# Scores of two heads at once over half of TensorE's rows, w1's row factors applied after the product, and filler products ahead of gelu

## The chip, the cores and the metric

One core of a Trainium2 chip runs the kernel. The metric is the device time of one execution in microseconds, median of several runs; the core's span in the profile is 1.7 to 2.9 us shorter. A run on one core has no die to compare with, so "fast" means within 1.5% of the fastest run of the same kernel.

## The reference, cut to what matters

```python
B, S, D, H, F = 1, 2048, 640, 32, 1536            # 32 heads of 20 columns
xn = layernorm(A_x)
q, k, v = heads(xn @ wqkv)
p = softmax(q @ k^T * 20**-0.5)                    # 32 x 2048 x 2048 exponentials
s = concat(p @ v) @ wo
h  = gelu(layernorm(xn) @ w1)                      # branch B, tanh gelu
x1 = xn + shift(h) @ w2                            # four column groups shifted by 1, -1, 2, -2 rows
g  = silu(x1 + gelu(layernorm(x1) @ w3) @ w4)
return A_x + s * g
```

The 32 x 2048 x 2048 exponentials are nearly all of the work. ScalarE takes most of them, in tiles of 128 x 1024; VectorE takes the rest by a bit trick on 16-bit integers (the "blocks" below).

## The kernel before: what the change and the argument touch

The kernel's instruction order is fixed when it is built. A planner walks through time; each task has an engine, a booked duration and a due time, and a ready task is put where the engine's booked time is free. Each engine is then given its list in that order.

TensorE's products here are of a column mode (128 rows, 32 columns; `128*32` or `128*22` in the profile) or of a row mode (32 rows, 128 columns; `32*128`). In the trace of the kernel before, a column group of four matmuls starts about 0.215 us after another one (though one matmul lasts 0.38 us by its modelled end), but 0.31 to 0.32 after a row-mode score; and two column groups ahead of a row-mode score need 0.55 us where two take 0.43. These extra times, about 0.11 us on entry and 0.10 on exit, are what "drain" stands for. The planner books what a change of mode costs:

```python
self.mode_cost = 100.0
...
            t.finish = st + t.dur
            if e == "pe":
                if t.mode != pe_mode:          # charged on entry and on exit
                    t.finish += self.mode_cost
                pe_mode = t.mode
...
def c_pe(ninstr, N):
    return ninstr * max(14.0, 0.106 * N)       # four column matmuls of 512: 217 ns
```

The scores of one ScalarE tile (two heads, 128 keys, 512 queries) are, from the second group on, eight column matmuls against zero-padded queries QM. They are booked at 440 ns. Each tile is followed by one exponential:

```python
        def fn(e):
            for jj in range(2):
                ...
                for c in range(4):
                    ins = e.matmul(out[32*c:32*c+32, :], self.KT[:, b, 128*kt + 32*c:128*kt + 32*c + 32],
                                   self.QM[:, gb, 2*a + jj, :], ..., tile_position=(0, 32 * c))
        T("pe", 220 if gb is None else 440, fn, ..., mode=int(gb is None), cls=-1, acq=("S", hs))
        return self.exp_act(hs, sa)
```

Before w1's products the kernel multiplies the whole transposed input by the row factors, one VectorE instruction of 5 x 516 columns for each of four chunks. The products are then copied out of PSUM:

```python
            T("dve", c_dve(KC * 516, "1x"), fy, ..., name=f"y2_{ch}")
            ...
                T("dve", c_dve(512), lambda e: e.tensor_copy(hx[:, ch, m, :], self.wbank(h)[:, 0:512]), ...)
```

`DUE` holds due times of the side work (projections, branch B), and `ND` says how many blocks of each group of 512 queries VectorE takes. Both were tuned for this planner.

## Time and profile before

| | before |
|---|---|
| time, median of 4 (range) | 890.98 us (888.92 to 891.34) |
| exponentials on ScalarE | 836 |
| first one starts, last one ends, tail | 36.3, 878.1, 11.3 us |
| granted TensorE clock, mean | 0.992 |

The lines that carry it are in the prediction below.

How to read ScalarE's rate: neighbouring exponentials overlap (one lasts 1036 ns in the profile). The busy time of their group counts overlap once, so busy time over count (779.9 / 836 = 0.933 us) is what one costs on average. If an exponential comes a little late, the overlap shrinks and the busy time per exponential grows, while the idle column shows nothing; the changed kernel below has 24.8 us of this.

### The profile page before, as it was taken

The page shows a single profiled execution, that of the slowest core. Times are in us where ns is not written, and L with a number is a line of the kernel's source. Part 1 is how long each engine was busy: PE and PEld are TensorE (multiplying, and loading weights), DVE is VectorE, ACT ScalarE, POOL GpSimd, SP SyncE. Part 2 cuts the span into 40 slices and gives each one's busy share as a digit, 9 for nine tenths or more (in the row PEclk, how much of TensorE's full clock was granted, in tenths as well). Part 3 has the DMA queues.
Part 4 walks back from the last instruction along what each step waited for, and adds up shares of the span by engine and source line. Part 5 has one row for each costly group of instructions (what it writes and reads, how often), then busy time and mean ns, then how long its engine had stood idle before and what let it go on. Part 6 is the DMA issues. An engine that isn't in the chain of part 4 may idle for free.

```text
span 889.4 us, 34152 instructions
## 1 busy us (share of the span) xinstructions
PE 829.2 (93%) x15630; PEld 364.1 (41%) x15630; DVE 724.4 (81%) x1000; ACT 851.0 (96%) x900; POOL 37.8 (4%) x69
## 2 busy tenths in 40 slices
PE   4999999999999999999998999999999799998996
PEld 2434333334444433344443544433434344444453
DVE  7756888887888899989776779987878679797895
ACT  6899999999999999999998999999999999999994
POOL 7310000000000000000000000000000000010000
PEclk9999999999999999999999999999999999999998
DMA  6003300012210013222223031222222201114322
GB/s 222 11 14 87 94 22 25 25 43 77 80 48 29 22 46 86 62 61 57 62 53 98 20 95 35 72 84 59 54 60 51 82 10 53 47 53 126 105 63 76
DMA packets 83548, 54.81 MB, mean 62 GB/s; under 512 B 52556, under 2 KB 77340, under 8 KB 83276
## 3 DMA queue, kind: packets, MB, share of 16 engines
q1 hardware_dynamic: 83404, 52.62, 21.1%
q8 instruction: 123, 2.02, 0.9%
q14 instruction: 21, 0.17, 0.1%
HBM read 37.91 MB, written 10.63 MB: 55 GB/s over the span
## 4 chain that ended last, share of the span: by engine, by line
ACT 45%; PE 27%; DVE 19%; DMA 8%; issue 1%; SPq 0%
ACT arena L1404 42%; PE psum L771 11%; PE psum L1380 8%; DVE arena L1345 4%; DVE arena L1431 4%; DMA arena<-recips 4%; PE psum L1362 3%; PE psum L1319 3%; PE psum L1354 2%; DMA recips<-arena 2%; DVE arena L970 2%; DMA queries<-arena 1%; ACT arena L1756 1%; ACT arena L1698 1%; DVE arena L1682 1%
## 5 line engine op out<-in xcount | busy, mean ns | idle before, releaser
L1404 ACT ACTIVATE arena<-psum 128x1024 bf16<-128x1024 f32 x836 | 779.9, 1036 | 16.5 <-PE psum L1362 5.6
L1380 PE MATMUL psum<-arena 128*32 128x512 bf16 x4992 | 380.0, 381 | 11.5 <-ACT arena L1404 9.5
L771 PE MATMUL psum<-arena 128*32 128x320 bf16 (+1 forms) x5952 | 360.3, 335 | 7.8 <-DVE arena L1161 3.5
L1431 DVE TENSOR_SCALAR arena<-psum 128x1024 uint16<-128x1024 f32 x188 | 229.1, 1218 | 52.9 <-PE psum L1362 51.8
L1345 DVE TENSOR_SCALAR arena<-arena 128x4096 uint16<-128x4096 uint16 (+1 forms) x236 | 230.1, 1008 | 5.4 <-PE psum L1354 4.1
L771 PEld LDWEIGHTS psum<-arena 128*32 128x32 bf16 x5952 | 147.9, 97 | 148.0 <-issue 27.4
L1380 PEld LDWEIGHTS psum<-arena 128*32 128x32 bf16 x4992 | 106.8, 95 | 145.6 <-ACT arena L1404 102.6
L1319 PE MATMUL psum<-arena 128*22 128x512 bf16 x1672 | 161.6, 381 | 2.0 <-DVE arena L1466 1.7
L1354 PE MATMUL psum<-arena 128*22 128x512 bf16 x1504 | 123.3, 380 | 2.1 <-DVE arena L1345 1.9
L1362 PE MATMUL psum<-arena 32*128 32x512 bf16 x800 | 83.7, 386 | 14.3 <-ACT arena L1404 6.6
L1319 PEld LDWEIGHTS psum<-arena 128*22 128x22 bf16 x1672 | 42.4, 92 | 54.2 <-issue 7.5
L1362 PEld LDWEIGHTS psum<-arena 32*128 32x128 bf16 x800 | 21.4, 91 | 98.8 <-ACT arena L1404 81.7
L1354 PEld LDWEIGHTS psum<-arena 128*22 128x22 bf16 x1504 | 36.4, 92 | 45.5 <-DVE arena L1345 10.6
L1753 DVE CAST arena<-psum 128x512 bf16<-128x512 f32 x48 | 33.0, 687 | 14.1 <-PE psum L771 14.1
L1205 DVE CAST arena<-psum 128x512 bf16<-128x512 f32 x40 | 27.3, 685 | 18.1 <-PE psum L771 18.1
L1479 DVE TENSOR_TENSOR arena<-arena 128x512 bf16<-128x512 f32 x28 | 19.3, 689 | 16.1 <-DMA arena<-recips 15.8
L1550 DVE SCALAR_TENSOR_TENSOR arena<-psum,arena 128x320 bf16<-128x320 f32 x32 | 15.5, 487 | 15.4 <-PE psum L771 15.4
L970 DVE BATCH_NORM_STATS2 arena<-arena 128x6 f32<-128x320 bf16 x52 | 23.0, 482 | 2.8 <-DMA arena<-in_A_x_dram 2.8
L1466 DVE COPY arena<-psum 128x512 f32<-128x512 f32 x28 | 19.2, 687 | 3.6 <-PE psum L1354 2.8
L1767 DVE TENSOR_TENSOR arena<-psum,arena 128x320 bf16<-128x320 f32 x32 | 15.5, 485 | 6.8 <-PE psum L771 6.8
L1756 ACT ACTIVATE arena<-arena 128x12288 bf16<-128x12288 bf16 x2 | 20.9, 10444 | 0.0
L1069 PE MATMUL psum<-arena 128*32 128x128 bf16 x320 | 9.3, 246 | 12.2 <-DVE arena L984 11.8
(101 smaller groups left out, 281.2 us busy)
## 6 DMA issues: line engine op xcount, KB each, us to landing
arena<-in_B_w_dram SPq DMA_DIRECT2D x48, 160.0 KB, 2.6
arena<-recips SPq DMA_DIRECT2D x28, 256.0 KB
arena<-arena SPq DMA_DIRECT2D x124, 32.0 KB, 1.9
arena<-in_B_w_dram SPq DMA_DIRECT2D x4, 960.0 KB, 5.3
arena<-in_A_x_dram SPq DMA_DIRECT2D x8, 320.0 KB, 6.1
arena<-in_A_x_dram SPq DMA_DIRECT2D x16, 160.0 KB, 2.5
out_dram<-arena SPq DMA_DIRECT2D x16, 160.0 KB, 1.8
arena<-keys SPq DMA_DIRECT2D x28, 80.0 KB
```

What stands on the lines that cost most here:

```text
L771: ins = e.matmul(pb[32 * c:32 * c + 32, 0:N], lhsT(k, c), rhs(k, c), start=(k == 0), stop=(stop and k == nk - 1), tile_position=(0, 32 * c))
L970: lambda e, li=li, n=n, hh=hh: e.bn_stats(st[:, li, 6 * hh:6 * hh + 6], xn[:, n, hD * hh:hD * hh + hD]),
L1205: T("dve", c_dve(512), lambda e, h=h, c=c: e.tensor_copy(KS[:, 512 * c:512 * c + 512], self.wbank(h)[:, 0:512]), reads=[wa], writes=[A("KS ...
L1319: ins = e.matmul(pb[32 * i:32 * i + 22, 0:512], VA[:, ql, kts[i // 2], i, :], PT[:, slots[i // 2][0].slot, 512 * (i % 2):512 * (i % 2) + 512],
L1345: T("dve", c_dve(w, "4x"), lambda e, v=v, dst=dst: e.tensor_scalar(dst, U[:, ub, 0:w], 0.5, EXP_B[v], op0=ALU.mult, op1=ALU.add), reads=ha ...
L1354: ins = e.matmul(pb[32 * i:32 * i + 22, 0:512], wv, dst[:, at:at + 512].bitcast(BF16), start=first, stop=final, tile_position=(0, 32 * i))
L1362: return e.matmul(out, self.KT[32 * i:32 * i + 32, b, 128 * kt:128 * kt + 128], self.QT[32 * i:32 * i + 32, b, 512 * qc:512 * qc + 512], s ...
L1380: ins = e.matmul(out[32 * c:32 * c + 32, :], self.KT[:, b, 128 * kt + 32 * c:128 * kt + 32 * c + 32], self.QM[:, gb, 2 * a + jj, :], start ...
L1404: lambda e: e.activation(self.PT[:, hp.slot, :], self.psum[:, 512 * hs.slot:512 * hs.slot + 1024], AF.Exp, scale=cfg.scale),
L1431: ins = e.tensor_scalar(U[:, ub, 1024 * at + 512 * k:1024 * at + 512 * k + w], self.psum[:, 512 * hd.slots[k]:512 * hd.slots[k] + w], a_ex ...
L1753: T("dve", c_dve(512), lambda e, h=h, fc=fc, i=i: e.tensor_copy(GT[:, i, fc, :], self.wbank(h)[:, 0:512]), reads=[wa], writes=at, name=f"g ...
L1756: T("act", 2750 + c_act(2 * FC * 512), lambda e: e.activation(GT[:, :, :, :], GT[:, :, :, :], AF.Gelu_apprx_tanh), reads=gta, writes=gta, ...
```

## The change

Its intent: halve the matmul time of ScalarE's scores by running two heads at once, each over 64 of the 128 rows; take the four long row-factor products off VectorE by multiplying when w1's products are evicted anyway; keep TensorE's clock up around the gelus with 24 filler products (before, the stretch from 702 to 710 us, after the third gelu, has a granted clock of 0.79); move more blocks to VectorE and some layer-norm tiles to GpSimd. The planner's bookings of transfers and of mode switches are altered, and all due times are retuned. Left out of the cut below are other booked times of transfers, the places of the blocks in groups with four of them (`UNITS`), and the loading of the row factors, which is now one transfer of 256 KB for each of the 20 evictions in place of one of 1 MB. Cut to its core:

```diff
-                if t.mode != pe_mode:
+                if pe_mode and not t.mode:              # a switch is charged on leaving a row mode only
                     t.finish += self.mode_cost
...
-        self.dma_bw = 280.0
+        self.dma_bw = 223.0
-            k0=-37.9, k1=-9.1, ...                      # all due times
+            k0=216.0, k1=-160.6, ...
+        self.POOLN = [6, 7, 8, 12]                      # norm tiles on GpSimd
-        self.FALL = False
+        self.FALL = True
+        self.FILL = 8                                   # fillers ahead of each of three gelus
-            [2, 2, 3, 3], [3, 3, 3, 3], ...             # ND: 94 blocks on VectorE
+            [1, 2, 3, 3], [3, 3, 3, 4], ...             # 101 blocks
...
+    def score_half(self, b, qc, kt, a, gb):
+            for jj in range(2):
+                r = slice(64 * jj, 64 * jj + 64)
+                ins = e.matmul(self.bank(hs.slot + jj)[:, :], self.KT[r, b, 128 * kt:128 * kt + 128],
+                               self.QM[r, gb, a + 2 * jj, :], ..., tile_position=(64 * jj, 0))
+        T("pe", 220, fn, ..., mode=1, cls=-1, acq=("S", hs))
...
-            T("dve", c_dve(KC * 516, "1x"), fy, ...)
-                T("dve", c_dve(512), lambda e: e.tensor_copy(hx[...], self.wbank(h)[:, 0:512]), ...)
+                T("dve", c_dve(512), lambda e: e.tensor_tensor(hx[...], self.wbank(h)[:, 0:512], RR[:, r, :], op=ALU.mult), ...)
+        self.fill("g1", at)                             # 8 x 16 matmuls, also ahead of the two gelus of w3
```

## The prediction

> **What bounds the kernel now.** I read the page's busy shares first, then its slices, then the groups by line and shape, then the waits, the chain of waits in order of time, and last a close timeline of TensorE.
>
> ```profile
> span 889.4 us, 34152 instructions
> PE 829.2 (93%) x15630; PEld 364.1 (41%) x15630; DVE 724.4 (81%) x1000; ACT 851.0 (96%) x900; POOL 37.8 (4%) x69
> ...
> PE   4999999999999999999998999999999799998996
> ...
> ACT  6899999999999999999998999999999999999994
> ```
>
> ScalarE is the bound: 96% busy, and full in all but the first two slices and the last. TensorE reads 93%, but matmul ends are modelled with the pipeline's tail, so its real slack must come from a timeline.
>
> ```profile
> L1404 ACT ACTIVATE arena<-psum 128x1024 bf16<-128x1024 f32 x836 | 779.9, 1036 | 16.5 <-PE psum L1362 5.6 <-PE psum L1319 5.1 <-PE psum L1380 4.2
> L1380 PE MATMUL psum<-arena 128*32 128x512 bf16 x4992 | 380.0, 381 | 11.5 <-ACT arena L1404 9.5
> L1431 DVE TENSOR_SCALAR arena<-psum 128x1024 uint16<-128x1024 f32 x188 | 229.1, 1218 | 52.9 <-PE psum L1362 51.8
> L1345 DVE TENSOR_SCALAR arena<-arena 128x4096 uint16<-128x4096 uint16 x140 | 167.5, 1226 | 3.0 <-PE psum L1354 2.3
> ```
>
> These are groups (busy us, mean ns, then idle before them). The 836 exponentials last 1036 ns each but overlap: 779.9 / 836 = 0.933 us apiece. With ScalarE's other late work (gelu 8.7 + 20.9, tanh 10.1, six table loads of 1.28 = 7.7, all from the groups) the list after the first exponential is 828.2 us. The first exponential starts at 36.3 (timeline), the last ends at 878.1 (ScalarE is busy for 3.1 of the window 875 to 880), so 11.3 us of tail follow. 36.3 + 828.2 + 11.3 = 875.8; the other 13.6 us are waits of ScalarE in the middle, close to the 14.9 that the group line gives to TensorE's lines. These are what a schedule can win back, and I want to know what causes them.
>
> ```profile
> 126.29 2.75 DVE arena L1682
> 129.04 1.14 DVE arena L1345
> 130.18 1.13 DVE arena L1431
> 131.32 0.17 DVE arena L1473
> 131.49 0.02 issue
> 131.50 3.08 DMA recips<-arena
> 134.58 0.02 issue
> 134.59 5.06 DMA arena<-recips
> 139.66 0.02 issue
> 139.68 0.69 DVE arena L1479
> ```
>
> This is the chain in order of time (start, length). VectorE, which runs its list in order, does a 2.75 us row-factor product (L1682), then its list stands until a reciprocal has gone out to memory and come back; ScalarE then misses 0.6 and 0.2 us near 144. The same two transfers stand ahead of its gaps near 193, 476, 586 and 656. In total VectorE loses this much to them:
>
> ```profile
> DVE arena L1479 <- DMA arena<-recips: 15.8, 12, 3.9
> ```
>
> [...]
>
> ```profile
> 50.31 0.39 PE L1362 MATMUL psum<-arena 32*128 32x512 bf16 x2
> 50.63 0.62 PE L771 MATMUL psum<-arena 128*32 128x512 bf16 x8
> 51.18 0.39 PE L1362 MATMUL psum<-arena 32*128 32x512 bf16 x2
> 51.49 0.40 PE L1319 MATMUL psum<-arena 128*22 128x512 bf16 x4
> 51.72 0.39 PE L771 MATMUL psum<-arena 128*32 128x512 bf16 x4
> ```
>
> Four column matmuls of 512 take about 0.215 us start to start. Two row matmuls side by side need 0.31 to 0.32 before the next column group starts (50.31 to 50.63), and two column groups ahead of a row group need 0.55 instead of 0.43 (50.63 to 51.18). One visit to a row mode thus costs about 0.11 on entry and 0.10 on exit. [...] TensorE waits 3.5 us before 696.9, and the granted clock of the window 702 to 710 is 0.79.
>
> **The change part by part.**
> Scores. A tile was 8 column matmuls, two rounds of four, 0.43 us; 624 of them are 268 us. Now it is two matmuls over 64 rows side by side, one round of 0.21, but in a row mode. In the built order 520 of the 592 such tiles stand alone between column work, and row-mode visits go from 210 to 751. Cost: 592 x 0.21 + 541 x 0.22 = 243 us. The halving of the matmul time is given back to drains: a lone tile costs 0.21 + 0.21 = 0.42 against 0.43. TensorE gains 25 us, mostly because there are 32 fewer such tiles.
> Added on TensorE: 16 more row groups of the shared tiles (3.4), 21 more value groups (21 x 0.215 = 4.5), 24 fillers of 16 matmuls (96 x 0.215 = 20.6). Sum +28.5: TensorE's work is a few us more, not less. Gelu waits for the last filler, but they are laid between scores ahead of it, so they cost slots, not a block.
> Exponentials. The blocks given to VectorE go from 94 to 101, so ScalarE has 14 fewer exponentials: 14 x 0.933 = 13.1 us, straight off the path. This is the largest sure gain.
> VectorE. 14 more evictions (17.1), 20 more wide pieces (20 x 1.226 = 24.5), 16 fewer narrow ones (16 x 0.689 = 11.0), four row-factor products of 2.83 gone (-11.4), two norm tiles gone (-0.9). Sum +18.3: 743 us, about 85% of the new span. The factor itself is free: it rides on an eviction that reads PSUM anyway (0.69 us either way).
> Prologue. 15 fewer value groups of 320 columns (0.137 each, 2.05 us) stand before the first score, where TensorE is nearly solid. Four norm tiles go to GpSimd, which may delay its own last powers. I take 1.3 us of the 2.05: first exponential at 35.0.
> Schedule. The planner's times for the small transfers and the bandwidth are corrected, and the big lump on VectorE is gone. The five stall sites named above sum to about 6 us (0.75, 0.7, 2.5, 0.4, 1.5); I expect most of it to go.
>
> **The sum.** Waits in the middle: 13.6 - 6 (transfers, lump) - 1.5 (clock near the third gelu) + 3.5 (VectorE and TensorE are denser) = 9.6. Then 35.0 + (828.2 - 13.1) + 11.3 + 9.6 = 871.0 us of span; the timed median is 1.3 above the profiled span before, so 872. I lean 1 us lower, as the due times were retuned with everything else: 871.
>
> **Rivals.**
> First, TensorE becomes cheaper than I say, because a switch to 64 rows drains less than one to 32 rows. For it: the planner now charges the switch on leaving only. Against it: the drain before 51.18 is on entry. If only 0.32 us were paid per tile, TensorE would gain 60 us, the waits would fall to about 5, and the time to about 866.
> Second, VectorE takes over as the bound. Counting the built order from the 200th to the 418th exponential (means as above, less 0.06 for the overlap of neighbours), VectorE has about as much work as ScalarE's 203 us there, from long runs with four blocks per group; before, the same count for exponentials 251 to 420 gives 91%, which matches 92% busy in 300 to 400. Against it: at 95% busy from 300 to 340 ScalarE lost nothing. If it bites, waits grow by 8 or so and the time is about 880.
> Third, TensorE is the bound, since nothing was taken from it and the span shrinks. By the same count it needs 48.4 us for exponentials 101 to 150, where ScalarE takes 46.7, and 50.7 against about 50.5 for 451 to 500. That would cost 3 to 6 us: 875 to 878.
>
> **Range and chances.** The floor with no waits at all is 35.0 + 815.1 + 11.3 + 1.3 = 863; the second and third rival together give about 884. Eight times in ten within 862 to 882. The line for "faster by over 2%" is 872.9, close to my sum, so it is little better than even: 0.55 faster, 0.43 the same, 0.02 slower.
>
> **What would show it right or wrong.** The exponentials: 822 at about 0.933, ScalarE near 837 busy. The half-row tiles: about 0.42 us from the start of such a tile's predecessor's end to the next column group, and TensorE's in-stream load not lower; if the next column group starts 0.21 after one, I was wrong on the drains. VectorE's waits for the reciprocals should fall well below 15.8. The clock at the gelus should stay near 1. VectorE's busy share between 230 and 430 us should be over 95%; if ScalarE's idle time sits there, the second rival is right. The prediction is wrong altogether if the first exponential starts later than before, or if ScalarE's waits in the middle rise above 13.6.

## More of the kernel before

Booked times that are wrong do not break the result. They produce an order that fits another machine.

One more view is needed as a measure for later, the share of each engine in the chain of waits that ended last:

```profile
ACT 45%; PE 27%; DVE 19%; DMA 8%; issue 1%; SPq 0%
```

ScalarE leads the chain. TensorE and VectorE each hold it for part of the span.

## The result, and the profile after

The changed kernel takes 917.82 us (914.84 to 919.08, four runs) against 890.98. The ratio is 1.030, with a 95% interval from 1.027 to 1.033: slower by 3%. All ratios here are those of the mean times of fast runs and not of the medians quoted beside them.

The page of the changed kernel (busy shares, three engines' slices, chain of waits by engine, the group of the exponentials):

```profile
PE 833.8 (91%) x12354; PEld 285.9 (31%) x12354; DVE 744.3 (82%) x1018; ACT 860.7 (94%) x884; POOL 44.7 (5%) x74
...
PE   4899999999899999988989999898996898989996
...
ACT  5799999999999999999999999899999899999995
...
PE 67%; ACT 24%; DVE 5%; DMA 3%; issue 1%; POOL 1%; SPq 1%; ACTq 0%
...
L1444 ACT ACTIVATE arena<-psum 128x1024 bf16<-128x1024 f32 x822 | 791.6, 1033 | 27.7 <-PE psum L1398 8.6
```

ScalarE still looks full, yet the chain has turned from ScalarE to TensorE (27% before, 67% after). TensorE's total busy time hardly moved (829.2 to 833.8). The group line explains where the time is: 822 exponentials take 791.6 us, 0.963 each instead of 0.933. At the old rate they would have taken 766.8.

The span grew by 23.7 us in the profiled runs. In terms of these lines: the first exponential starts 1.1 later (37.4); 14 exponentials fewer save 13.1; the stretched busy time costs 791.6 - 766.8 = 24.8; idle time ahead of exponentials rises by 11.2; the tail is 0.5 shorter. The sum is +23.5.

So the larger loss does not show as idle time at all. To see it I counted, from the trace's start times, the interval from one exponential to the next where nothing lies between them on ScalarE. Back to back it is 903 to 905 or 919 to 921 ns (584 of the 824 intervals before, 396 of 810 after), and never less than 903. Before, 128 intervals lie between 0.96 and 1.10 us; after, 340 do. I call these "small late" ones. All that intervals of up to 1.10 us have above 0.925 sums to 11.3 us before and to 40.9 after: 29.6 us of waits of which the page shows few as idle. What longer gaps have above 0.925 went from 18.5 to 22.3. The granted clock does not explain the small late ones: by the trace's clock records TensorE ran at half clock for 17 us between the first and the last exponential (7 us before), and none of the 340 lies there.

Where they come from is seen in TensorE's timeline (start, length, instruction; L1388 is a row-mode score, L1398 a half tile, the other lines are column work):

```profile
62.75 0.39 PE L1388 MATMUL psum<-arena 32*128 32x512 bf16 x2
63.07 0.83 PE L782 MATMUL psum<-arena 128*32 128x512 bf16 x12
63.84 0.39 PE L1388 MATMUL psum<-arena 32*128 32x512 bf16 x2
64.15 0.40 PE L1345 MATMUL psum<-arena 128*22 128x512 bf16 x4
...
153.93 0.39 PE L1398 MATMUL psum<-arena 64*128 64x512 bf16 x2
154.25 0.83 PE L782 MATMUL psum<-arena 128*32 128x512 bf16 x12
155.01 0.39 PE L1398 MATMUL psum<-arena 64*128 64x512 bf16 x2
155.33 0.40 PE L1345 MATMUL psum<-arena 128*22 128x512 bf16 x4
```

From one score to the next it is 1.09 and 1.08 us: 0.32 for the score and the switch behind it, then three column groups and the switch ahead of the next score, 0.76. ScalarE could have taken the next tile after 0.91. The planner booked 0.22 + 0.10 for such a tile, and three groups at 0.217: 0.97. It believed that three groups nearly fit into the time of one exponential. They don't. Of the 399 exponentials that start over 0.95 us after the one before, I found the score of 393 to be a row-mode tile with TensorE's work solid up to it.

### The profile page after: what moved, and what is told of

Read it like the earlier page. It is cut to its first block, busy times and chain, and to the rows that moved or that the text cites. A ratio compares the mean times of both kernels' runs of the same rounds, so it can differ in the third digit from the quotient of the medians.

```text
span 913.1 us, 27675 instructions
## 1 busy us (share of the span) xinstructions
PE 833.8 (91%) x12354; PEld 285.9 (31%) x12354; DVE 744.3 (82%) x1018; ACT 860.7 (94%) x884; POOL 44.7 (5%) x74
## 3 DMA queue, kind: packets, MB, share of 16 engines
q1 hardware_dynamic: 86336, 56.82, 22.3%
## 4 chain that ended last, share of the span: by engine, by line
PE 67%; ACT 24%; DVE 5%; DMA 3%; issue 1%; POOL 1%; SPq 1%; ACTq 0%
PE psum L782 25%; ACT arena L1444 19%; PE psum L1398 15%; PE psum L1345 10%; PE psum L1380 8%; PE psum L1388 6%; PE psum L1749 2%; DVE arena L1471 2%; DMA arena<-in_B_w_dram 2%; ACT arena L1810 1%; ACT arena L1738 1%; DMA arena<-in_A_x_dram 1%; ACT arena L1826 1%; DMA queries<-arena 0%; ACT arena L1016 0%
## 5 line engine op out<-in xcount | busy, mean ns | idle before, releaser
L1444 ACT ACTIVATE arena<-psum 128x1024 bf16<-128x1024 f32 x822 | 791.6, 1033 | 27.7 <-PE psum L1398 8.6
L782 PE MATMUL psum<-arena 128*32 128x320 bf16 (+1 forms) x5952 | 348.9, 336 | 6.0 <-DMA arena<-in_B_w_dram 1.4
L1471 DVE TENSOR_SCALAR arena<-psum 128x1024 uint16<-128x1024 f32 (+1 forms) x204 | 246.5, 1209 | 61.2 <-PE psum L1388 60.0
L1371 DVE TENSOR_SCALAR arena<-arena 128x4096 uint16<-128x4096 uint16 (+1 forms) x244 | 247.0, 1036 | 6.8 <-PE psum L1380 5.8
L1398 PE MATMUL psum<-arena 64*128 64x512 bf16 x1184 | 230.7, 387 | 10.1 <-ACT arena L1444 9.3
L782 PEld LDWEIGHTS psum<-arena 128*32 128x32 bf16 x5952 | 139.4, 96 | 122.2 <-issue 49.9
L1380 PE MATMUL psum<-arena 128*22 128x512 bf16 x1616 | 128.9, 381 | 0.6 <-DVE arena L1371 0.5
L1398 PEld LDWEIGHTS psum<-arena 64*128 64x128 bf16 x1184 | 56.6, 92 | 216.3 <-ACT arena L1444 119.4
L1388 PE MATMUL psum<-arena 32*128 32x512 bf16 x864 | 90.4, 385 | 31.6 <-ACT arena L1444 26.3
L1388 PEld LDWEIGHTS psum<-arena 32*128 32x128 bf16 x864 | 23.1, 91 | 109.3 <-ACT arena L1444 77.2
L1380 PEld LDWEIGHTS psum<-arena 128*22 128x22 bf16 x1616 | 34.2, 90 | 35.7 <-issue 16.8
L1749 PE MATMUL psum<-arena 128*32 128x512 bf16 x384 | 25.1, 381 | 0.5 <-DVE arena L1225 0.5
L1286 DVE CAST arena<-psum 128x320 bf16<-128x320 f32 x32 | 15.4, 488 | 8.8 <-PE psum L782 8.7
L1519 DVE TENSOR_TENSOR arena<-arena 128x512 bf16<-128x512 f32 x28 | 19.1, 684 | 2.8 <-DMA arena<-recips 2.7
L1089 PE MATMUL psum<-arena 128*32 128x128 bf16 x320 | 8.9, 247 | 13.4 <-DVE arena L999 10.6
```

The source lines that it names most:

```text
L782: ins = e.matmul(pb[32 * c:32 * c + 32, 0:N], lhsT(k, c), rhs(k, c), start=(k == 0), stop=(stop and k == nk - 1), tile_position=(0, 32 * c))
L1371: T("dve", c_dve(w, "4x"), lambda e, v=v, dst=dst: e.tensor_scalar(dst, U[:, ub, 0:w], 0.5, EXP_B[v], op0=ALU.mult, op1=ALU.add), reads=ha ...
L1380: ins = e.matmul(pb[32 * i:32 * i + 22, 0:512], wv, dst[:, at:at + 512].bitcast(BF16), start=first, stop=final, tile_position=(0, 32 * i))
L1388: return e.matmul(out, self.KT[32 * i:32 * i + 32, b, 128 * kt:128 * kt + 128], self.QT[32 * i:32 * i + 32, b, 512 * qc:512 * qc + 512], s ...
L1398: ins = e.matmul(self.bank(hs.slot + jj)[:, :], self.KT[r, b, 128 * kt:128 * kt + 128], self.QM[r, gb, a + 2 * jj, :], start=True, stop=Tr ...
L1444: lambda e: e.activation(self.PT[:, hp.slot, :], self.psum[:, 512 * hs.slot:512 * hs.slot + 1024], AF.Exp, scale=cfg.scale),
```

## The experiments

Theories, and what each would show:

- **Booking.** The planner charges a row-mode visit 0.10 us and the chip takes 0.21. The order then carries one column group too many in many slots, and each such slot costs 0.1 to 0.17 us.
- **Load.** TensorE simply has more to do: fillers, value groups, mode switches.
- **Half tiles.** The half tile is dearer than the column tile on the chip.
- **VectorE.** 101 blocks are too many; ScalarE waits for what VectorE frees late.
- **Order.** Any re-made order is worse until its due times are tuned for it.

The last one matters for every experiment here: each edit re-plans the whole program. So there are controls for it, and kernels whose due times and block shares were searched anew. For that search, orders were rated off the chip with durations taken from these traces; only chip times are told. The searches were not all equally long: some 6,000 to 7,000 orders for r1, r3, r5 and r7, 11,000 for r2, 13,000 for r9 and r10, 18,000 for r8. For r6 none is given. The expectations of r1, r3 and r7 say that they were searched as long as r2; by these counts they were not.

All runs in one table. "us per exp." is the group's busy time over its count, "small late" as above. Each ratio is against the kernel before on the same chip.

| run | us, median (range) | ratio (95%) | exps. | us per exp. | small late | first exp. |
|---|---|---|---|---|---|---|
| before | 890.98 (888.92-891.34) | 1 | 836 | 0.933 | 128 | 36.3 |
| after | 917.82 (914.84-919.08) | 1.030 (1.027-1.033) | 822 | 0.963 | 340 | 37.4 |
| e1_cost | 911.91 (910.88-915.21) | 1.024 (1.022-1.026) | 822 | 0.931 | 108 | 37.5 |
| e2_col | 924.31 (920.87-926.98) | 1.036 (1.033-1.040) | 822 | 0.944 | 193 | 38.1 |
| e3_nofill | 928.08 (925.71-928.48) | 1.041 (1.039-1.043) | 822 | 0.962 | 337 | 38.3 |
| e4_before_cheap | 910.8 (909.92-912.38) | 1.022 (1.021-1.024) | 836 | 0.956 | 313 | 36.2 |
| c2_replan | 907.54 (905.85-908.8) | 1.018 (1.016-1.020) | 836 | 0.933 | 123 | 35.4 |
| e5_before_half | 909.81 (906.62-911.66) | 1.021 (1.018-1.023) | 836 | 0.927 | 104 | 36.9 |
| e6_half_cheap | 930.03 (929.12-931.68) | 1.044 (1.042-1.046) | 836 | 0.960 | 315 | 35.9 |
| e7_nd | 955.48 (954.42-957.56) | 1.073 (1.070-1.075) | 836 | 0.966 | 334 | 38.6 |
| r1_fill | 910.12 (909.18-911.22) | 1.020 (1.015-1.025) | 838 | 0.929 | 117 | 41.8 |
| r2_nofill | 888.87 (885.18-890.96) | 0.996 (0.990-1.002) | 830 | 0.928 | 113 | 41.2 |
| r3_col | 893.67 (892.51-896.13) | 1.002 (0.996-1.009) | 834 | 0.932 | 132 | 39.9 |
| r5_half | 887.64 (886.34-889.39) | 0.995 (0.990-1.000) | 846 | 0.927 | 124 | 37.2 |
| r7_cheap | 912.38 (911.46-913.5) | 1.024 (1.022-1.026) | 826 | 0.960 | 329 | 36.6 |
| r8_pool | 881.16 (880.71-881.79) | 0.989 (0.987-0.990) | 826 | 0.927 | 110 | 38.7 |
| r6_best | 887.16 (883.63-888.8) | 0.995 (0.993-0.997) | 834 | 0.930 | 124 | 37.9 |
| r9_before | 889.9 (886.71-892.57) | 0.996 (0.993-0.999) | 836 | 0.933 | 128 | 36.1 |
| r10_half | 883.07 (881.63-883.74) | 0.989 (0.986-0.991) | 844 | 0.926 | 125 | 36.1 |

### The booking alone, in the kernel before

The sharpest test leaves the chip's instructions as they were and tells the planner a wrong price. A column score tile, which takes 0.43 us, is booked at 0.33:

```diff
 # before
-        T("pe", 220 if gb is None else 440, fn,
+        T("pe", 220 if gb is None else 330, fn,
```

> The kernel before, nothing changed on the chip's work, but the planner books a column score tile at 0.33 us in place of 0.44. Booking theory: this alone makes it slower by 2 to 4 per cent, 905 to 925 us, with TensorE solid before most late scores. Load theory and VectorE theory: the work of every engine is the same, so within 1 per cent of 891.

It is 2.2% slower, with 313 small late exponentials instead of 128. TensorE's timeline around the same place, first the kernel before, then this one (L1380 is a column score tile, L1319 and L1354 are value products):

```profile
62.30 0.60 PE L1380 MATMUL psum<-arena 128*32 128x512 bf16 x8
62.73 0.39 PE L1319 MATMUL psum<-arena 128*22 128x512 bf16 x4
62.95 0.39 PE L1354 MATMUL psum<-arena 128*22 128x512 bf16 x4
63.16 0.60 PE L1380 MATMUL psum<-arena 128*32 128x512 bf16 x8
```

```profile
62.28 0.60 PE L1380 MATMUL psum<-arena 128*32 128x512 bf16 x8
62.71 0.39 PE L1319 MATMUL psum<-arena 128*22 128x512 bf16 x4
62.93 0.60 PE L1354 MATMUL psum<-arena 128*22 128x512 bf16 x8
63.36 0.60 PE L1380 MATMUL psum<-arena 128*32 128x512 bf16 x8
```

Between two scores the right booking puts two groups of four, and the next score starts after 0.86 us. The short booking puts three, and it starts after 1.08. This is the same 1.08 as in the changed kernel, without any half tile in the program. The chain of waits of this run turns in the same way as that of the changed kernel:

```profile
PE 48%; ACT 35%; DVE 12%; DMA 5%; issue 1%; SPq 0%
```

A re-planned order could be worse for any reason, so a control changes the booking by next to nothing:

```diff
 # before
-        self.mode_cost = 100.0
+        self.mode_cost = 104.0
```

> Control: the kernel before, with the planner's charge for a mode change at 104 ns in place of 100 and nothing else. No engine gets more or other work; only the static order falls out anew, without the due times being retuned for it. If an order that is merely not retuned costs as much as the runs so far lost, this is 900 to 912 us, with few long gaps of ScalarE (over 1.1 us start to start) and not with many small late exponentials; if re-planning is harmless, within 1 per cent of 891.

This costs 1.8%, nearly as much as the wrong booking. It loses it in another way: 123 small late exponentials, as before, but the idle time ahead of exponentials rises from 16.5 to 32.9 us, a single gap near 524 us holding 10.1 of it. So two costs have to be kept apart. A wrong price shows as hundreds of small late exponentials; an untuned order shows as a few long gaps. The time alone can't tell them apart, the counts can.

### The booking put right in the changed kernel

```diff
 # after
-                if pe_mode and not t.mode:
+                if t.mode != pe_mode:
```

> The changed kernel, with one line of the planner undone: it charges 0.10 us on entering a row mode and on leaving it, as before, so a lone half-row tile is booked at 0.42 us and not 0.32. Booking theory (the planner puts about 0.1 us too much column work between two score tiles, so scores come late although TensorE's total is unchanged): most of the loss comes back, 875 to 898 us, exponentials start to start 0.92 to 0.95 us on average away from gaps, fewer than 250 late ones. Load theory (TensorE simply has too much in-stream work, with the drains and fillers): the work is the same, so 910 to 920. VectorE theory (seven more blocks): 910 to 920.

The small late exponentials fall from 340 to 108, and an exponential costs 0.931 us again:

```profile
L1444 ACT ACTIVATE arena<-psum 128x1024 bf16<-128x1024 f32 x822 | 764.9, 1049 | 44.5 <-PE psum L1345 34.5
```

Busy time is down by 26.7 us. But idle time ahead of the group went from 27.7 to 44.5, in four gaps of 3.4 to 7.7 us above all, and the tail grew from 10.9 to 17.3. Only 6 us of the time came back. So the time, 911.9, fell in the range of the load theory (910 to 920) and not in that of the booking theory (875 to 898); only the count came out as the booking theory had it. A reading that fits both is that the due times of the changed kernel had been tuned on the wrong price; the searched kernels below test it.

### Half tiles, in the kernel before and taken out of the changed one

```diff
 # e5: before, plus score_half and the order of heads as in the change, planner as before
+                    if col:
+                        heads = (0, 2, 1, 3)
+                        slots = [self.score_half(b, qc, x, a, gb) for a in range(2)]
 # e6: the same, with the change's price
-                if t.mode != pe_mode:
+                if pe_mode and not t.mode:
 # e2: after, with column tiles
-        self.ROWK = [[0, 1, 2, ..., 15], ...]
+        self.ROWK = [[], [], [], [], []]
```

> The kernel before with half-row tiles in place of the column tiles and nothing else; its planner charges the mode on entering and leaving, so a lone tile is booked at 0.42 us. Booking theory: the swap is neutral, 884 to 898 us. If the half-row tile itself is what hurts (drains, a longer way to the first exponential), 905 to 920. If it helps because tiles share visits, below 880.

> The kernel before with the half-row tiles, now booked as the change books them (mode change charged on leaving only, 0.32 us for a lone tile). Against the same kernel booked at 0.42 (909.8 us, 104 small late exponentials): booking theory: the small late ones rise above 300 and the time is 912 to 925, although the chip's work is the same; if only the lack of retuning matters, the small late ones stay near 100.

> The changed kernel with all of ScalarE's tiles as eight column matmuls again (booked 0.44 us, which is what they take), everything else as changed. Booking theory: 875 to 898 us, as when the half tiles are booked rightly. Load theory with drains as the culprit: row-mode visits fall back to about 220, but the in-stream work is nearly the same by my count (0.43 against 0.42 per tile), so 905 to 920; if the drains cost more than I count, it falls to 890. VectorE theory: 910 to 920, as the blocks stay 101.

e5 and e6 have the same instructions and differ only in the price: 909.8 and 930.0 us, 104 and 315 small late ones. e5 missed the booking theory's 884 to 898. It is still no verdict on the half tile, since it is as much slower as the control c2 and has long gaps where that has them (8.2 and 3.4 us ahead of silu near 525). e2, without half tiles, is slower still, at 924.3 us and above what any theory gave it. It too is an order that nobody tuned, so it shows only that taking the half tiles out did not help; whether they are free is for r2, r3 and r5.

### Fillers and blocks

```diff
 # e3: after
-        self.FILL = 8
+        self.FILL = 0
 # e7: after, ND of the kernel before (94 blocks)
-            [1, 2, 3, 3], [3, 3, 3, 4], ...
+            [2, 2, 3, 3], [3, 3, 3, 3], ...
```

> The changed kernel without the 24 filler products (20.6 us of TensorE). Load theory: TensorE's work bounds it, so nearly all of the 20 us come back, 895 to 902. Booking theory: the fillers were booked at what they cost, so the slots stay overbooked: 906 to 918, and the small late exponentials (start to start 0.96 to 1.10 us) stay above 250 of the 822.

> The changed kernel with the 94 blocks of before in place of 101 (14 more exponentials, 12.8 us of ScalarE at 0.911 each; VectorE about 30 us less). VectorE theory: the wait of ScalarE falls by more than the exponentials cost, so 895 to 910. Booking theory: not faster, 915 to 940, as VectorE was not what made the scores late and the due times now fit even less.

Both are slower, 928 and 955 us, above the range of either theory, with the small late ones about as many as in the changed kernel (337 and 334 against 340). If load alone or a full VectorE were the cause, less of either would have helped. But both are also orders nobody tuned, so by themselves they only fail to support these theories. Part of their loss is the clock: by the clock records TensorE ran at half clock for 48 us in e3 and 61 us in e7, against 17 us in the changed kernel, and the intervals in or just after these stretches have 10.6 and 15.8 us above 0.925, against 2.4. A view of the changed kernel speaks more plainly on VectorE, which in the stretch from 230 to 430 us has most of its work (200 us; PE, PEld, DVE, ACT, POOL busy; clock; DMA):

```profile
230.00:430.00 200.00, 185.96 (x2736) 62.55 (x2727) 182.43 (x266) 194.36 (x197) 5.56 (x9) 1.00 0.20 53
430.00:630.00 200.00, 189.37 (x2864) 66.50 (x2864) 168.69 (x207) 190.98 (x188) 1.01 (x1) 0.99 0.23 60
```

VectorE is 91% busy in the first stretch, and ScalarE loses less there than in the second, where VectorE has more room: counted by intervals, so that small waits are in it, 13.5 us above 0.925 against 17.1.

### The same, with due times searched anew

To separate the price from the tuning, fillers and price were crossed, each with due times and block shares searched for it. Two of the four are r1 and r2 (right price, with and without the 24 fillers); r7 has the change's price and no fillers; the changed kernel itself is the fourth, as tuned by its author.

```diff
 # r1, r2, r3: e1_cost with searched due times and ND
+        # r1: FILL = 8 (93 blocks)    r2: FILL = 0 (97 blocks)    r3: FILL = 0, column tiles (95 blocks)
 # r7: after with FILL = 0, searched, price left as in the change (99 blocks)
```

> The same with the 24 fillers kept, searched anew as long (93 blocks). If the fillers only cost their 20.6 us of TensorE in a schedule that has little slack: 8 to 18 us slower than without them. If they keep the clock up and that is worth more: as fast or faster than without them, with the granted clock above 0.99.

> The changed kernel, half-row tiles booked at 0.42 us, no fillers, and the due times and block counts (97 blocks) searched anew for an order that suits the durations of the traces. Booking-and-retuning theory (the parts are sound, the loss came from an order made for a TensorE that does not exist): faster than before, 868 to 886 us, under 140 small late exponentials and less than 12 us of long gaps. If the half-row tile or the extra blocks themselves cost, it stays above 895.

> The same without fillers and with column tiles in place of half-row tiles, searched anew as long (95 blocks). By my count a lone half-row tile is no cheaper (0.42 against 0.43 us), so the half-row version should lead only by what tiles that share a visit and the smaller number of instructions give: 0 to 10 us. If half-row tiles are really cheaper, more than 12 us slower than them.

> The changed kernel without fillers, with its own booking (the row switch charged only on leaving, about 0.1 us too little for a score tile), but with due times and block shares searched anew over as many orders as the two earlier searched kernels without fillers (r2_nofill with honest booking: 888.9 us, 113 exponentials with a start-to-start interval of 0.96 to 1.10 us). Booking theory: no search over due times can mend a slot that is booked too short, so it stays at 898 us or more, with over 250 such small late exponentials. Retuning-only theory (the 29 us were only due times that did not fit): at most 892 us, small late ones between 100 and 150.

| searched or tuned | 24 fillers | no fillers |
|---|---|---|
| charged on leaving only | 917.8 (after) | 912.4 (r7) |
| charged both ways | 910.1 (r1) | 888.9 (r2) |

r2 had about twice the search of r1 and r7, so the differences to it are upper ends. With the right price and no fillers the slowdown is gone, though r2 missed its 868 to 886 by 3 us and its long gaps held 18.8 us and not under 12. The search did not mend the short price: r7 keeps 329 small late exponentials at 0.960 us each. The exponentials of r7 and of r2:

```profile
L1444 ACT ACTIVATE arena<-psum 128x1024 bf16<-128x1024 f32 x826 | 792.7, 1033 | 22.2 <-PE psum L1398 6.7
```

```profile
L1444 ACT ACTIVATE arena<-psum 128x1024 bf16<-128x1024 f32 x830 | 770.6, 1054 | 17.8 <-PE psum L1345 8.2
```

The price is worth up to 912.4 - 888.9 = 23.5 us without fillers. The fillers cost up to 910.1 - 888.9 = 21.2 us once the price is right. The two overlap: alone, either repair gives 5 to 8 us.

The fillers' own matmul time is 24 x 4 x 0.215 = 20.6 us, so at the upper end they went into the time whole. The two traces tell 16.8 of the 19.1 us between their spans: r1 leaves ScalarE 8 exponentials more (93 blocks instead of 97; 8 x 0.929 = 7.4 us), its long gaps hold 7.3 us more, its tail 1.5 and its start 0.6. The number of blocks was the search's choice, so not all of this need be the fillers' doing. Nor did they raise the clock beyond what runs vary by: its mean is 0.984 to 0.988 in r1's runs and 0.982 to 0.989 in r2's, where over 0.99 was expected.

r2 against r3 puts half tiles 4.8 us ahead of column tiles, in kernels that are otherwise the same but for their searched times and block shares (97 and 95) and the length of the search. The intervals of their ratios to before overlap.

Half tiles alone, added to the kernel before, searched:

```diff
 # r5: e5_before_half with searched due times and ND (89 blocks)
```

> The kernel before with half-row tiles booked at 0.42 us and nothing else of the change, due times and block counts searched anew (89 blocks). Booking-and-retuning theory: the 18 us that it lost without retuning come back, 882 to 896 us, so the half-row tile is neutral. If the tile costs in itself, it stays at 905 or more.

It is at 887.6 us, level with the kernel before to slightly faster: with times and block shares searched, the half tile is no loss.

### The norm tiles on GpSimd

In the changed kernel and in r1 and r2 the first exponential is late. r8 is r2 with the four norm tiles back on VectorE and ScalarE, r6 the same with FALL off as in the kernel before, both searched:

```diff
-        self.POOLN = [6, 7, 8, 12]
+        self.POOLN = []
+        # r8: FALL = True (99 blocks)    r6: FALL = False (95 blocks)
```

> Honest booking, no fillers, no layer-norm tiles on GpSimd, searched anew; otherwise as r2_nofill. If GpSimd's slow norm tiles hold back the first exponential: it starts at 35 to 37 us instead of 41.2, and the time is 880 to 887 us. If something else holds it back (the lump of transfers at the start): it stays above 39.5 us and the time at 886 to 891.

> As r8_pool, and also without the option that lets a score pair straddle the two bank pairs (FALL, off in the kernel before). Everything I believe costs time is gone: booking honest, no fillers, norm tiles on VectorE, due times searched. If my account is complete it beats both kernels: 876 to 886 us, ratio 0.985 to 0.995, first exponential at 35 to 37 us, under 130 small late exponentials. If the half tiles or the factors on w1's products carry a cost that I have not found, it stays within 0.3% of the kernel before or above it.

In the changed kernel the same instruction, by line and shape, on the two engines:

```profile
L999 DVE TENSOR_SCALAR arena<-arena 128x640 bf16<-128x640 bf16 x24 | 9.5, 437 | 0.0
L999 POOL TENSOR_SCALAR arena<-arena 128x640 bf16<-128x640 bf16 x2 | 5.1, 2547 | 0.0
```

GpSimd needs 2.5 us for what VectorE does in 0.44, a subtraction and a multiplication by per-row operands. Its other two norm tiles, of the same size but with a multiply and an add, took 0.87 and 1.36 us (a mean of 0.87 in r1, r2 and r7). Spans on GpSimd are rough, so the factor of near six is too; the runs without these tiles are the test. The planner booked 160 + 0.86 x 640 = 710 ns. Without them the first exponential starts at 38.7 and 37.9 us, 2.5 to 3.3 us earlier than in r2, though not at the 35 to 37 expected, so they are part of the delay and not all of it. r7, which has them, starts at 36.6, so how late the first exponential is depends on the order as well. r8 is 7.7 us faster than r2; it had also been searched for longer, and I can't split the two.

r8 beats both kernels: 881.2 us, ratio 0.989 to before. By a line of 2% that is still the same time, but the interval leaves out 1. Its exponentials in the page:

```profile
L1445 ACT ACTIVATE arena<-psum 128x1024 bf16<-128x1024 f32 x826 | 766.0, 1061 | 14.2 <-PE psum L1346 6.8
```

It has 10 exponentials fewer than the kernel before, at 0.927 us each, and less idle time ahead of them.

r6 was expected to be the best and is not: 887.2. FALL off was worth nothing, or its search ended in a worse place.

### Is the gain the change's, or the search's?

```diff
 # r9: before, only its due times searched
 # r10: before plus half tiles, charged both ways, searched as long as r9 (90 blocks)
```

> A control for the search itself: the kernel before, nothing changed but its due times, searched anew over as many orders as r8_pool had. If the gain of r8_pool (881.2 against 891.4) is only the search, this gains as much: 880 to 884 us. If it is the change's parts (half tiles, the factor on w1's products, more blocks on VectorE) that the search only makes usable, the kernel before has nothing left to find: 888 to 893 us, ratio 0.997 to 1.002.

> The kernel before with half tiles honestly booked and due times searched twice as long as r5_half (887.6). If half tiles alone, with a good order, give what r8_pool gives: 880 to 884 us. If r8_pool needs the other parts (factor on w1's products, blocks moved to VectorE): 885 to 889 us.

The expectation says that r9 was searched as long as r8; it was 13,000 orders against 18,000, and as long as r10. The search found nothing to speak of in the kernel before: 889.9 us, at a ratio of 0.996 (the kernel before itself varied from 887.7 to 898.6 on that chip). Half tiles alone take it to 883.1, ratio 0.989, as good as r8, and 0.8% below r9:

```profile
ACT 72%; PE 15%; DVE 9%; DMA 4%; issue 0%; POOL 0%; SPq 0%; DVEq 0%
...
L1424 ACT ACTIVATE arena<-psum 128x1024 bf16<-128x1024 f32 x844 | 781.8, 1059 | 6.3 <-PE psum L1378 2.7
```

This kernel has 844 exponentials, 8 more than before, and is still faster, because the idle time ahead of them fell from 16.5 to 6.3 us and an exponential costs 0.926. ScalarE leads 72% of the chain. So of the parts of the change the half tile is the one that most likely pays, at about 1%. It is not shown to pay by itself, because r9 is not a full control: r9 kept its 94 blocks where they were, while r10's block shares were searched too (90 blocks), and 13 of r9's 37 due times are still the old ones, so its search may have stayed near where it began. A kernel before with searched block shares was not run. The factors on w1's products and the extra blocks, which r8 has besides, add nothing that these runs can show, and r1 and r2, with the GpSimd tiles and in r1 the fillers, are slower than r8. Why the half tile pays is not settled: 577 of its 636 tiles stand alone between column work, where one takes TensorE as long as a column tile (in the two traces 0.32 to the next group and 0.11 ahead of it, against 0.43). A candidate is that a score is finished 0.2 us sooner after its bank comes free. Where TensorE stood waiting for an exponential to free the bank, a lone column tile ended 0.67 us after that exponential (22 tiles of the kernel before) and a lone half tile 0.45 us after it (31 tiles of the changed kernel), ends as the profile models them. No run isolates what this is worth.

## Why the prediction was wrong, point by point

The prediction was 871 us, within 862 to 882, and the time was 917.8.

**Number of exponentials: right.** 822, as counted from the built order.

**Price of an exponential, and the waits in the sum: the failed step.** The prediction used 0.933 as ScalarE's own rate, and then, in the sum, "+ 3.5 (VectorE and TensorE are denser)". The runs showed that the rate is not ScalarE's own: back to back it is 0.904 to 0.921, and the 0.933 already held some 11 us of small waits for scores. Taking it for a rate hid these waits. In the changed kernel the stretch grew by 24.8 us and the idle time by 11.2, 36.0 in all, where the prediction had a net fall of 4 (13.6 to 9.6). Its own signs of being wrong altogether, a later first exponential and more waits, both came true. The term meant for TensorE's density was too small by a factor of about ten. (The parts listed for ScalarE's 828.2 us add up to 827.3; the 13.6 us of waits are the remainder, so the slip cancels in the sum.)

**What was overlooked.** The cause stood in the diff: the planner's charge on leaving only, against a cost that the prediction itself measured at 0.11 on entry and 0.10 on exit. The prediction named both, but used the line only as evidence for a rival (perhaps the chip is cheaper than I think). The other reading, that the chip is as measured and the planner is therefore wrong in 751 visits, was not followed. It was enough to compare one slot: 0.97 booked, 1.08 by the prediction's own numbers, 0.91 for ScalarE.

**Sum over TensorE: right and useless.** "+28.5" against 25 saved gave a few us more, and the busy time rose by 4.6. But equal totals say nothing when the work is dealt out in slots of 1.08 and others below 0.9: no exponential starts less than 0.903 after the one before, so one delayed in one slot is not given back by the next.

**Half tiles: right.** 0.32 to the next column group, and 0.76 for three groups (0.645) and the 0.11 ahead of the next score: a lone tile costs about 0.43. In the changed kernel's timeline both steps are the same for scores of 32 rows and of 64.

**VectorE: right.** 743 predicted, 744.3 measured. Its waits for reciprocals fell as expected:

```profile
DVE arena L1519 <- DMA arena<-recips: 2.7, 4, 1.2
```

That is down from 15.8 us. These waits were part of the largest saving that the prediction named for the schedule. What their fall was worth no run isolates; TensorE held 67% of the chain by then. VectorE's share between 230 and 430 us was 91%, not over 95.

**First exponential: wrong.** Predicted 35.0, measured 37.4. The prediction took GpSimd's norm tiles for a possible small delay; two of the four cost 2.5 us each. They delay the start in r2 against r8, but r7 shows that the order has a part in it too.

**Clock at the third gelu: wrong.** The prediction gave the fillers 1.5 us, the author's estimate; that they would hold the clock up was not shown by any trace, and with them it fell further. They lie between scores, the last of them 2 us ahead of the gelu (696.2 to 706.6 us), and the idle time of TensorE comes during it and just after: 3.9 us up to 701.9 and 6.2 up to 709.0. The stretch from 700 to 720 us, first before, then after (columns as above):

```profile
700.00:720.00 20.00, 17.53 (x324) 7.89 (x316) 12.96 (x15) 18.62 (x20) 0.00 (x0) 0.91 0.17 54
```

```profile
700.00:720.00 20.00, 11.19 (x140) 3.88 (x140) 7.62 (x10) 17.90 (x13) 0.00 (x0) 0.66 0.16 51
```

The granted clock is 0.66 instead of 0.91. At the second gelu the clock records have 3.4 us at half clock in both kernels, at the third 3.4 before and 13.7 after. And "they cost slots, not a block" was right, but slots were what TensorE didn't have: r1 against r2 puts them at up to 21 us.

**The rivals.** The first (a cheaper switch) fell with the 0.32 and 0.11 us around a half tile, the second (VectorE) with the stretch from 230 to 430 us. The third, TensorE as the bound, pointed the right way, but at 3 to 6 us it was an average over stages of 50 exponentials, and the loss is inside single slots.

**What stays open.** In the 29 us between the changed kernel and r2 the price and the fillers overlap, so neither has one worth. In a comparison of kernels that were not searched, an untuned order can be worth as much as the 16 us of c2, the only control of this kind. Whether the half tile by itself gives the gain of r10, and why a lone one helps, is open too (see above).

## What to carry to other kernels

Where a planner fixes the order, check every price that a change touches against the trace before looking at sums: a price that is 0.1 us short in a task that recurs 600 times puts one piece too many into slot after slot, and in r7 a search over due times did not repair it. Read an engine's rate as the smallest interval between starts (here 0.903 us), not as busy time over count (0.933); the difference is waits that the idle column doesn't show. And compare an edited order only with orders that were tuned as long, or count a symptom (here the small late exponentials) that tuning doesn't move.
